# Windowed attention and a feed-forward layer on one core: batch 0 begun in groups of 256 tokens, two head pairs stacked on the partitions

## The chip, the cores and the metric

One core of a Trainium2 chip runs the whole program. Its engines work beside each other, each on its own instruction stream: PE (TensorE, matrix products and transposes), DVE (VectorE), ACT (ScalarE), POOL (GpSimd) and SP, which only issues transfers. ACT and POOL issue transfers as well. The metric is the device time of one execution in microseconds, as the median of several runs.

## The reference

There are 4 batches of 8 heads with 768 tokens and 64 numbers per head. A token sees itself and the 127 before it, and the first four tokens ("sinks"). The result goes through a layer of 512 to 2048, a squared relu, and back to 512.

```python
scores = scale * np.matmul(q, k.transpose(0, 1, 3, 2))
rel = pos[:, None] - pos[None, :]
keep = (pos[None, :] < 4) | ((rel >= 0) & (rel < 128))
scores = np.where(keep, scores, -1000000000.0)
a = np.exp(scores - np.max(scores, axis=-1, keepdims=True))
a = a / (np.sum(a, axis=-1, keepdims=True) + 1e-09)
x = np.matmul(a, v).transpose(0, 2, 1, 3).reshape(B * S, H * D)
out = np.maximum(x @ w_in, 0.0) ** 2 @ w_out
```

## The kernel before, in words

The kernel keeps both weight matrices in on-chip memory as bf16 and goes through the four batches one after the other. Within a batch the work is cut into groups of tokens (GROUPS, lines 323 to 325: batch 0 has one group of 512 and one of 256 tokens), and within those into stretches of 256 tokens (s = 0, 1, 2). Heads go in pairs (m = 0 to 3), so that two heads fill 128 partitions.

For batch 0 the start runs like this:

- **Loads.** load_qk (line 328) loads one head pair's k or q for 512 tokens as one transfer of 256 KB in fp32, four tokens (1 KB) to a partition row, all on SP's queue; eight such transfers load the first group. The second group comes with load_cast (line 355) on POOL's queue, which turns it into bf16 on the way. load_v (line 372) and load_w_in (line 299) are on POOL's queue too. Line 417 loads the sink values (vs_in), for batch 0 on ACT's queue.
- **Regroup** (line 471): a cast to bf16 on DVE, ACT or POOL (tile qs).
- **Transpose** (line 488, matmuls on line 500): PE transposes 128x128 blocks into PSUM (tile pt). **Unload** (line 515): DVE or ACT copies them to qkT, and puts the tokens back in their order.
- **Scores** (line 590): for s = 0 a bias product (line 600) puts the mask in ahead of the products on line 607; ACT takes the exponential (line 628); for later s the mask is put on by DVE or POOL (line 633).
- **Values** (line 656, matmuls on line 676), **norm** on DVE (line 687), and the **bridge** (line 718): PE transposes the result, and DVE or ACT copies it to xT (line 734).
- **Layer 1** (line 746, matmuls on line 757) and layer 2 follow.

PE also runs matmuls whose result nobody reads (warm, line 178, matmuls on line 182). The table DUMMIES (line 56) says how many stand ahead of which operation, by the operation's number.

Every piece of work is an operation of a Plan, numbered in the order in which the code makes it. The text ORDER (lines 21 to 55) lists these numbers in the order in which they are handed to the engines, each with a letter for its engine (p PE, d DVE, a ACT, g POOL; none means the first that is named) and, behind a plus, a choice of buffer. The engines run their instructions strictly in this order and wait on semaphores for each other. The framework counts transfers of SP and ACT on eight semaphores in turn; an issue waits until the last transfer on its semaphore has landed.

The constants are made by fill (line 220), fill_first and fill_second (lines 232 and 235) on DVE and by build_ident, build_triangles, build_bias and build_head_rows (lines 238 to 264) on POOL.

Of the kernel before, what the change touches and what calls it, by code (L numbers as in the profile page):

```python
# [21 lines left out]
0 7 8 9 1 5 10 11 2 12 13 3 14 15 55d 57+0 16 19 59a 20 17 56d 21 18 61d 63+0 22 58 62d 65a 60d 64 6 67a 83+1 79 66a  # L22
68d 69+1 85 70 71d 103+0 84+0 105 73g 74d 72d 23 75+1 86 76 77d 91+0 78a 24 87+1 93 25 89 88 92+0 80 26 114+1 90 94
95+0 4 96 117 97 106g 99+1 98 104+0 107 100d 101 118g 81+1 102d 113+0 108d 156 115 127 27 28 29 30 31 32 33 34 35 36
37 38 116d 82 109+0 111 39 40 41 119+1 121 157a 158a 110 112 120 122 162 123+1 125 163d 168 169d 126a 124a 171 172a
170a 159 160d 177 128 131 165 173d 161d 132d 178d 166d 164a 130a 129a 133a 144 146 136 138 174 145 137 289 290 148
134 175a 140 135 176a 147d 167d 139d 291 179d 292 293 141d 142 143 149g 42 43 44 45 46 150 151 47 48 49 50 51 52 53
54 365 366 367 368 208g 369 370 371 372 373 294 295 152 154 296 153d 155d 297d 298d 186 187d 180 181a 200+0 204+1
192+0 201 193 205 194a 206d 195a 189 207d 182d 203a 196+0 197 183 198a 190a 191a 188d 199d 202d 274 212+0+0 184d 209
278 279 215 213 237+0+0 210+1 211 238 240 185d 300 301 275 214 302 241d 276 277 303 280 281 282 304 219+0+0 283 222  # L30
220 306a 305 307 230+0+0 309a 233 231 308 311 223 216 221 310 239d 224+0 312 234g 232g 299 385 386 384 383 313 225
314 242+0 217+0 243 218 284 315 316 235+0 236 285 251+0 286a 287a 317d 252d 253d 244+0 246 226+1 228 247d 227d 245a
248+1 229a 399 322 249d 250d 402 400 323d 355 401 256+0+0 259 257 340 254+0 255 341a 258d 358 356 342a 396 260d 334
335a 374 375 376 377 378 379 380 381 395g 388 390 387 288 392 391 318 389 393 394 331 263+0+0 332a 261+1 264 266 319
262 267d 324d 406 333a 407 320a 337 409 265g 382 597 268+0 598 599 600 601 602 603 604 605 606 607 608 609 610 338a
321d 403 269 328 627d 410 270+0 272 404 408 329a 271a 273d 359 325 405 339a 336a 326a 346 347d 357 327a 415 418 419d
330d 352 411 353a 416 412 354d 447 448 343 344a 345a 349 422 423 425 417g 426g 611 451 452 397 363 449 453d 350d 398
450 351a 348a 454 455 457 466 456a 438 458 459 441 439 467 485 486 489 490 487 460 488 461 361 492 431 491a 432 434
615 413 616 622 620 619 493 462 494d 468 463 464a 414 465 621 617 618 420 440g 612 424g 427 496 433g 442g 428 498
421 470 471 443 435g 436 472a 504a 495 362 499 497 500 473 444 437 508 505 469 628 501 475d 474 477 647 429 625 445  # L40
430 446 650 502a 648 624 503 623 626 360 476 478 481 507 479 506 480 364 482 483d 523+0 525a 524 631 527 526 528 634
632 509+0 510 529 511d 512 530 531a 654 538 633 539 513 514 515 655 533 534 657 649g 656g 516 517a 638 613 614 535
635 536d 537 641 519 520 532a 636 658g 651g 521 639 569+0 570 637 571a 629 583+0 630 572 573 585a 640 522a 518a 574
584 587 575 576 586 555+1 642 589 577a 588 643 679 557a 540 556 590 559 591a 592a 578a 558 560 579 580 593 594 581
561 562 595 541+0 542 683 563a 564a 543d 545 544 680 546 565 547 566 548 684 686 644 567 685a 596a 549a 582a 681
550d 689 682 645 484 646 670 551 552 687 690 673 671 674g 553 688a 554a 663 691 694 666 664 665g 568d 698 692 693
699 659 652 702 703 705 667g 672g 695 696d 700 653 717 660 718 721 668 697 661 736a 704a 669 737 675 676 701 722 739
740 738 708 677 678 662 755+1 706 709 741+1 742 757a 719 720 756 743a 723a 707d 759 745 724 758 761 725 744 760 762
763a 764a 711 746 727 710 713 726a 765 766 747 712 769 714 771 767 728 730 715d 772 748 749a 729 815+0 816 817a 732
770 731 818 733 819 751 752 787+1 734a 735 716 801+0 802 803a 789a 753 820 804 768d 821 788 822 773+1 805 791 754a  # L50
823a 824a 775a 790 806 750d 792 829 807 774 793 776 825 808 794 826 809a 827 830 831 795a 796a 810a 777 779 811 778
812 797 798 833 780 834 836 813 799 828a 835a 781a 832 838d 839 783 784 782a 800a 814a 837 840 841 844 785 786d 842
848 849 852 853 855 843 845 846d 867 854a 850 851 858 857d 868 871 847 856 859 873a 861 862 860 863 864 869 872 865a
866 870 877 874 876a 875 878 880 881 886 879 882 883 885 884
# [59 lines left out]
def kernel(  # L114
# [112 lines left out]
    def fill_one(i):  # L227
        nc.vector.memset(kblk[i], 0.0)
        nc.vector.memset(vs_sb[i], 0.0)
        nc.vector.memset(v_sb[i][:, :, :, D:D + 1], 1.0)  # L230
# [4 lines left out]
    def fill_second(e):  # L235
        fill_one(1)

# [28 lines left out]
    bias_slot = Slot("sg", 4)  # L266
    c_const = op(-9, {"dve": 0.85}, fill, takes=[bias_slot])
    c_fill = op(-8.9, {"dve": 0.95}, fill_first, after=[c_const])
# [30 lines left out]
    def load_w_in(i, behind=None, yields=()):  # L299
        c = slice(512 * i, 512 * i + 512)  # L300
        w_in_op[i] = dma_op(
            "pool", ("w_in", i),
            lambda e: [nc.gpsimd.dma_start(out=w_in_sb[:, i],
                                           in_=moe_w_in[:, c].rearrange("(a p) f -> p a f", p=128))],
            2.6, behind, yields=yields)
        w_in_op[i].margin = 0.4 + 0.4 * i
# [17 lines left out]
    GROUPS[0] = [(0, 4), (512, 2)]  # L324
    GROUPS[1] = [(0, 4), (512, 2)]
    ROW = {512: 0.03, 1024: 0.052}

    def load_qk(b, m0, ti, g, pairs=2, behind=None, yields=()):


        t0, n = GROUPS[b][g]
        shares = 4 // pairs if n == 2 else 2 if pairs == 1 else 1
        half, share = m0 // pairs % shares, ("share", b, g, ti, m0 // (pairs * shares))
        if not half:
            qr_slot[share] = Slot("qr", 4 if n == 2 and pairs == 1 else 2)
        for m in range(m0, m0 + pairs):
            qr_slot[b, m, ti, g] = qr_slot[share]

        def run(e):
            if half == 0:  # L340
                qr_t[share] = bank(qr_slot[share], "qr", [128, shares * 2 * pairs, n * D], FP32)
            t = qr_t[share][:, 2 * pairs * half:2 * pairs * half + 2 * pairs, :]
            qr_t[b, "all", m0, ti, g] = t
            for m in range(m0, m0 + pairs):
                qr_t[b, m, ti, g] = t[:, 2 * (m - m0):2 * (m - m0) + 2, :]
# [6 lines left out]
        for m in range(m0, m0 + pairs):  # L352
            ops["qk", b, m, ti, g] = o
# [931 lines left out]
```

## Time and profile before

| | us |
|---|---|
| median of the runs | 213.04 |
| the runs | 213.04, 212.20, 213.47 |
| the profiled execution | 211.87 |
| its span, first to last instruction | 210.17 |
| mean granted clock of PE | 0.997 |

Line 2 of the next block is PE's busy share in 40 equal slices of the span, in tenths (9 is 90% or more); the others are DVE, ACT and POOL in the same way.

```
PE   3999999999999999999999999799999999999993
DVE  7487567366999964789997988999989978999863
ACT  2498287407744579898952268889870244896110
POOL 7999774898877941999369023700253000000000
```

A line of the chain of waits has the start, the length and what ran; a line of the timeline has the start, the length, the engine, the source line and the tiles, and in brackets the idle time before it and what ended it. A "q" behind an engine's name means that its sequencer issued a transfer.

### The profile page before, as it was taken

What the parts mean: (1) busy time and instruction counts of PE and PEld (TensorE: products, weight loads), DVE (VectorE), ACT (ScalarE), POOL (GpSimd) and SP (SyncE); (2) the same over time, 40 slices, a digit from 0 to 9 for tenths busy, and PEclk for the clock granted to TensorE, in tenths of its full rate; (3) what the DMA queues carried; (4) which work ended last, traced back from release to release, by engine and by line L of the source; (5) the groups of instructions that cost most, each with busy time, mean ns of one, the idle gap of its engine ahead of it and who ended that gap; (6) DMA issues with size and microseconds to landing.
All of it is one profiled execution on the core that took longest, in us unless ns stands there. A gap on an engine that the chain in (4) does not pass through costs nothing.

```text
span 210.2 us, 5719 instructions
## 1 busy us (share of the span) xinstructions
PE 201.4 (96%) x2383; PEld 169.4 (81%) x2383; DVE 170.8 (81%) x317; ACT 126.6 (60%) x162; POOL 101.8 (48%) x143
## 2 busy tenths in 40 slices
PE   3999999999999999999999999799999999999993
PEld 3859996689468845679789988699899999999892
DVE  7487567366999964789997988999989978999863
ACT  2498287407744579898952268889870244896110
POOL 7999774898877941999369023700253000000000
PEclk9999999999999999999999999999999999999998
DMA  5999999999999999999987639700512300400222
GB/s 171 278 188 206 171 201 214 161 155 205 153 112 157 104 150 252 138 124 144 149 102 151 103 77 179 50 3 0 150 62 69 75 5 38 166 0 0 103 100 100
DMA packets 93881, 26.09 MB, mean 124 GB/s; under 512 B 86816, under 2 KB 91552, under 8 KB 93856
## 3 DMA queue, kind: packets, MB, share of 16 engines
q0 software_dynamic: 69248, 12.59, 81.3%
q1 hardware_dynamic: 24424, 13.07, 27.9%
q8 instruction: 18, 0.29, 0.6%
q10 hardware_dynamic: 184, 0.07, 0.1%
q14 instruction: 7, 0.06, 0.1%
HBM read 27.30 MB, written 6.29 MB: 160 GB/s over the span
## 4 chain that ended last, share of the span: by engine, by line
PE 94%; DVE 2%; ACT 1%; POOL 1%; issue 1%; POOLq 0%; DVEq 0%
PE py L1086 29%; PE pm L757 20%; PE pm L887 17%; PE po L676 7%; PE py L976 7%; PE ps L607 6%; PE pt L500 3%; PE pt L182 2%; PE px L725 1%; ACT expm L628 1%; PE ya L1086 1%; PE ps L600 1%; PE pk L566 1%; DVE r L955 1%; DVE gT_sb L911 0%
## 5 line engine op out<-in xcount | busy, mean ns | idle before, releaser
L215 POOL TENSOR_SCALAR_AFFINE_SELECT expm<-expm 128x512 bf16<-128x512 bf16 x42 | 29.2, 724 | 49.5 <-ACT expm L628 24.5
L628 ACT ACTIVATE expm<-ps 128x1024 bf16<-128x1024 f32 (+1 forms) x48 | 43.8, 950 | 12.4 <-PE ps L607 11.3
L757 PE MATMUL pm<-xT,w_in_sb 128*128 128x256 bf16 (+1 forms) x320 | 44.7, 294 | 0.0
L757 PEld LDWEIGHTS <-w_in_sb 128*128 128x128 bf16 x320 | 34.2, 114 | 6.6 <-issue 0.9
L1086 PEld LDWEIGHTS <-gT_sb 128*128 128x128 bf16 x336 | 31.1, 98 | 4.2 <-issue 0.5
L1086 PEld LDWEIGHTS <-sg 128*128 128x128 bf16 x240 | 22.8, 98 | 3.3 <-issue 0.5
L768 ACT ACTIVATE r<-pm 128x1024 bf16<-128x1024 f32 x14 | 14.3, 1022 | 13.5 <-PE pm L757 13.4
L887 PEld LDWEIGHTS <-w_in_sb 128*128 128x128 bf16 x256 | 21.8, 114 | 0.5 <-issue 0.2
L887 PE MATMUL pm<-xs,wi 128*128 128x128 bf16 (+1 forms) x192 | 19.5, 246 | 1.5 <-DVE xs L845 0.9
L1086 PE MATMUL py<-wt,gT_sb 128*128 128x256 bf16 x160 | 20.8, 273 | 0.0
L1086 PE MATMUL py<-wt,sg 128*128 128x256 bf16 x160 | 20.6, 273 | 0.0
L909 ACT ACTIVATE gT_sb<-r 128x1024 bf16<-128x1024 bf16 x18 | 18.4, 1051 | 0.3
L1086 PE MATMUL py<-w_out_sb,gT_sb 128*128 128x256 bf16 x144 | 18.5, 273 | 0.0
L189 ACT ACTIVATE osb<-py 128x256 f32<-128x256 f32 (+1 forms) x15 | 6.2, 410 | 20.3 <-DMA out_dram<-osb 6.0
L770 DVE TENSOR_SCALAR r<-pm 128x1024 bf16<-128x1024 f32 x10 | 12.2, 1222 | 7.5 <-PE pm L757 4.3
L887 PEld LDWEIGHTS <-wi 128*128 128x128 bf16 x192 | 16.4, 113 | 2.2 <-issue 2.1
L693 DVE TENSOR_TENSOR xn_sb<-po,rc 128x512 bf16<-128x512 f32 (+1 forms) x28 | 17.2, 615 | 1.0
L676 PEld LDWEIGHTS <-expm 128*128 128x128 bf16 x352 | 16.3, 97 | 1.4 <-issue 0.5
L676 PE MATMUL po<-v,expm 128*128 128x65 bf16 x352 | 17.3, 193 | 0.1
L943 ACT ACTIVATE r<-pm 128x1024 bf16<-128x1024 f32 x12 | 12.1, 1021 | 8.1 <-PE pm L887 7.9
L928 DVE TENSOR_TENSOR t<-t,pm 128x512 f32<-128x512 f32 x24 | 15.9, 680 | 0.9 <-ACT t L189 0.4
L955 DVE CUSTOM_DVE_ANT_1 r<-pm,t 128x1024 bf16<-128x1024 f32 x12 | 14.5, 1220 | 1.6 <-PE pm L887 1.5
(97 smaller groups left out, 381.9 us busy)
## 6 DMA issues: line engine op xcount, KB each, us to landing
out_dram<-osb SPq DMA_DIRECT2D x11, 512.0 KB, 4.5
v<-in_v_dram POOLq DMA_DIRECT2D x24, 128.0 KB, 7.1
qn<-in_k_dram POOLq DMA_DIRECT2D x20, 128.0 KB, 7.1
qn<-in_q_dram POOLq DMA_DIRECT2D x20, 128.0 KB, 6.9
w_in_sb<-in_moe_w_in_dram POOLq DMA_DIRECT2D x4, 512.0 KB, 10.2
w_out_sb<-in_moe_w_out_dram POOLq DMA_DIRECT2D x4, 512.0 KB, 10.4
qr<-in_k_dram SPq DMA_DIRECT2D x4, 256.0 KB, 5.1
qr<-in_q_dram SPq DMA_DIRECT2D x4, 256.0 KB, 4.8
```

The costliest lines, as they stand in the source:

```text
L215: nc.gpsimd.affine_select(out=e_tile, in_=e_tile, compare_op=ALU.is_ge, fill=fill, base=i - 1, pattern=[[0, n], [1 if i else -1, 128]], ch ...
L628: nc.scalar.activation(out=x[:, :, o:512], in_=bank_t["s", b, s, m][:, :, o:512], func=AF.Exp, scale=scale)
L676: touch(("po", b, s, m0), e, nc.tensor.matmul(pv[:, i, h2, :], lhsT=lhsT, rhs=rhs, start=(n_ == 0), stop=(n_ == len(mms) - 1)), j)
L693: touch(("po", b, s, m0), e, nc.vector.tensor_tensor(out=xn_sb[:, 2 * s:2 * s + 2, 128 * (m0 + j0):128 * (m0 + j0 + nj)].rearrange("p i (j ...
L757: nc.tensor.matmul(pm[:, i, :], lhsT=w_in_sb[:, fb // 4, kb, fb % 4:512:4], rhs=xT[:, c0 // 256:(c0 + cw) // 256, kb, :], start=(kb == 0), ...
L768: nc.scalar.activation(out=o, in_=h, func=AF.Relu)
L887: touch(tag, e, nc.tensor.matmul(y[:, bk, i, :], lhsT=weights(name, f0 + i, a), rhs=rhs[:, a, :], start=fresh and i == 0 and a == 0, stop= ...
L909: nc.scalar.activation(out=d, in_=x, func=AF.Square)
L928: touch(tag, e, nc.vector.tensor_tensor(out=T["t"], in0=T["t"], in1=T["y"][:, bk], op=ALU.subtract), bk)
L955: touch(tag, e, nc.vector._custom_dve(TENSOR_ADD_SAT, out=r.rearrange("p b n c -> p b (n c)"), in0=T["y"].rearrange("p b n c -> p b (n c)" ...
L976: touch((b, u), e, nc.tensor.matmul(pm[:, i, :], lhsT=gT_sb[:, fb, 128 * t:128 * t + 128], rhs=w_out_sb[:, fb, :], start=(fb == 0), stop=( ...
L1086: ins = nc.tensor.matmul(y_, lhsT=x[:, i, :], rhs=r_, start=(first or tail and n == 2) and i == 0, stop=i == HB - 1, skip_group_check=not ...
```

## The change

- Batch 0 is cut in three groups of 256 tokens. The first two are loaded by a new load_qk: for two head pairs at a time, one pair goes to partitions 0 to 63 and the other to 64 to 127, as two transfers of 128 KB in 1 KB rows. For the first group one of the two is on SP's queue and the other on ACT's; for the second group both are on SP's.
- A regroup, a transpose and an unload now handle two head pairs of 256 tokens, where they handled one pair of 512. Their number for the first 512 tokens stays as it was.
- The second group of 256 tokens has its sink scores of its own; the first has none.
- The memset of the ones in v_sb[0] stands ahead of all other constants, and the loads of the values wait for it alone. They are the first thing that POOL issues.
- The values of s = 0 no longer wait for the sink values. vs_in of batch 0 is loaded on SP's queue.
- ORDER is new throughout. DUMMIES stays as it is, while the numbers of the operations change.

```diff
+    def fill_ones(e):
+        nc.vector.memset(v_sb[0][:, :, :, D:D + 1], 1.0)
...
+    c_ones = op(-9.1, {"dve": 0.2}, fill_ones)
     c_const = op(-9, {"dve": 0.85}, fill, takes=[bias_slot])
...
-    GROUPS[0] = [(0, 4), (512, 2)]
+    GROUPS[0] = [(0, 2), (256, 2), (512, 2)]
...
+    def load_qk(m0, ti, g):
+        t0 = GROUPS[0][g][0]
+        if not m0:
+            qr_slot[ti, g] = Slot("qr", 2)
+        for half in range(2):
+            def run(e, half=half):
+                if not m0 and not half:
+                    qr_t[ti, g] = bank(qr_slot[ti, g], "qr", [128, 2, 2, 4 * D], FP32)
+                h0 = 2 * (m0 + half)
+                return [(nc.scalar if half and not g else nc.sync).dma_start(
+                    out=qr_t[ti, g][64 * half:64 * half + 64, m0 // 2],
+                    in_=(q, k)[ti][0, h0:h0 + 2, t0:t0 + 256, :].rearrange("h (p t) d -> p h (t d)", t=4))]
...
-            o.after.append(c_rest if b else c_fill)
+            o.after.append(c_rest if b else c_ones)
...
                     def regroup(e, m=m, ti=ti):
+                        t = qs_t[b, m, ti, g] = bank(qs_slot[b, m, ti, g], "qs", [128, 4, 2, D], BF16)
+                        copy(e, t, qr_t[ti, g][:, m // 2].rearrange("p h (t d) -> p t h d", d=D))
...
                             ins = copy(e,
+                                       qkT_sb[:, m:m + 2, j, t0 // 128:last // 128, :].rearrange(
+                                           "c i a b -> c i (a b)").rearrange("c i (p t) -> c i p t", t=4),
+                                       bank_t[b, m, g][:, j, 0:512].rearrange("c (t i p) -> c i p t", t=4, i=2))
...
-                                + [A["sink_values"]] + prev_bridge)
+                                + ([A["sink_values"]] if s else []) + prev_bridge)
...
-    load_sinks("act", 0)
-    for m in range(NP):
-        for ti in (1, 0):
-            load_qk(0, m, ti, 0, 1)
-    for b in range(1, B):
+    for g in range(2):
+        for m0 in (0, 2):
+            for ti in (1, 0):
+                load_qk(m0, ti, g)
+    for b in range(B):
         load_sinks("sp", b)
-    load_v(0, 0, None, [("qk", 0, 3, 0, 0)])
+    load_v(0, 0)
...
             at(0, 0.0, 1.0, ("den", "att"))
...
-            at(1, 0.2, 0.725, "att")
+            at(1, 0.0, 1.0, ("den", "att"))
+            at(2, 0.2, 0.725, "att")
```

More of the change, by code (lines that the diff above doesn't have):

```diff
@@ L323 @@
     GROUPS = {b: [(0, 6)] for b in range(B)}
-    GROUPS[0] = [(0, 4), (512, 2)]
+    GROUPS[0] = [(0, 2), (256, 2), (512, 2)]
     GROUPS[1] = [(0, 4), (512, 2)]
[L326 to L345, printed above, removed]
-            return [nc.sync.dma_start(
-                out=t,
-                in_=(q, k)[ti][b, 2 * m0:2 * m0 + 2 * pairs, t0:t0 + 128 * n, :].rearrange(
-                    "h (p t) d -> p h (t d)", t=n))]
-        o = dma_op("sp", ("qk", b, m0, ti, g), run, 16 * pairs * ROW[256 * n] + (0.7 if (b, m0, ti, g) == (0, 0, 0, 0) else 0.0), behind,
-                   () if half else [qr_slot[share]], yields)
-        for m in range(m0, m0 + pairs):
-            ops["qk", b, m, ti, g] = o
@@ L495, in transpose @@
                             for ti in part:
[L496 removed]
+                                for t in range(nt):
                                     o = 128 * n * ti if w == 2 else 0
```

119 lines of the change are left out of this document (53 added, 66 removed).

## The prediction, made before the changed kernel ran

> **What bounds the kernel now.** I read the page first, for the share of each engine, then the busy time by stretch, then the chain of waits, and last the timeline of the first 17 us.
>
> ```profile
> span 210.2 us, 5719 instructions
> PE 201.4 (96%) x2383; PEld 169.4 (81%) x2383; DVE 170.8 (81%) x317; ACT 126.6 (60%) x162; POOL 101.8 (48%) x143
> ...
> 0.00:16.83 16.83, 13.13 (x178) 10.17 (x179) 11.55 (x33) 9.82 (x14) 14.63 (x30) 1.00 1.24 212
> 16.83:130.00 113.17, 113.17 (x1341) 89.45 (x1341) 89.88 (x165) 71.62 (x91) 75.84 (x99) 1.00 1.69 155
> 130.00:135.00 5.00, 3.46 (x57) 2.91 (x54) 4.82 (x6) 4.39 (x6) 5.00 (x8) 1.00 0.95 78
> 135.00:206.70 71.70, 71.67 (x816) 66.85 (x812) 64.50 (x114) 40.46 (x53) 6.28 (x9) 1.00 0.18 56
> 206.70:210.20 3.50, 0.00 (x0) 0.00 (x0) 0.01 (x1) 0.28 (x1) 0.00 (x0) 0.83 0.45 150
> ```
>
> In the rows by stretch the columns are the stretch, its length, and busy us of PE, PE's weight loads, DVE, ACT and POOL. PE never rests from 16.83 to 130 and from 135 to 206.7. Its idle time is 3.5 us ahead of its first instruction, 1.54 us between 130 and 135, and the 3.5 us of the last stores. So a change of the start is worth what it moves the moment from which PE never rests, which is the first product of layer 1 (16.83), if the same work is done by then.
>
> ```profile
> 3.53 2.95 PE pt L182 x26
> 6.48 0.43 PE pt L500 x4
> 6.91 1.40 PE pt L182 x18
> 8.30 0.45 PE pt L500 x8
> ...
> 16.83 1.91 PE pm L757 x16
> ```
>
> These are lines of the chain of waits (start, us, what). The first 26 matmuls are the dummies of line 182: 2.95/26 = 113 ns each. The eight transposes at 8.30 take 56 ns each. The 18 dummies between take 78 ns on average, so the granted clock doubled among them: about n x 107 + (18 - n) x 56 = 1400 gives n = 8, which is 7.7 us, 4.1 us after PE began. PE started early on work that nobody needs and had its full clock when the real transposes came in numbers.
>
> ```profile
> 0.82 0.46 SPq L346 DMA_DIRECT2D qr<-in_k_dram  x1
> ...
> 2.13 1.28 ACT L189 ACT_TABLE_LOAD   x1 [2.13 <-issue]
> ...
> 5.65 0.43 DVE L191 CAST qs<-qr 128x512 bf16<-128x512 f32 x1 [0.60 <-DMA qr<-in_k_dram]
> ...
> 7.06 0.45 DVE L191 CAST qs<-qr 128x512 bf16<-128x512 f32 x1 [0.99 <-DMA qr<-in_q_dram]
> ...
> 10.06 2.50 ACT L628 ACTIVATE expm<-ps 128x768 bf16<-128x768 f32 x3
> ```
>
> In the timeline the casts show when loads of 256 KB land: the first four start at 3.60, 4.63, 5.65 and 7.06. ACT's table is loaded by 3.41, in the shade of the loads, and the first exponential starts at 10.06.
>
> **The change, part by part.** *Same work ahead of layer 1.* The listing of the built program puts 32 transposes, 8 bias products, 40 score products, 24 value products, 8 bridge transposes and 4 sink products ahead of the first layer 1 product in both kernels. So the work behind it (186 us of PE plus 1.54 and 3.5) is the same, and the sum is: time after = time before + (new start of layer 1 - 16.83) + change in later stalls.
>
> *Dummies.* DUMMIES still names the old operations. In the new numbering 57, 63, 64, 83, 91 and 97 are loads, a regroup, norms and a copy, which call no warm; only 101 (3) and 119 (2) do. 58 of 63 dummies go. Their time itself (about 4.5 us at 107 and 56 ns) lay ahead of real work and costs nothing, but PE now begins with the first real transposes, at about 5.7. With the 4.1 us that the trace shows from first matmul to full clock, the full clock comes at 9.8, and until then a transpose takes 107 and not 56 ns.
>
> The Trainium skill (TensorE: Matmul & The Clock Gate, Part 1) has a free-running window of about 3.4 us that must be busy, which by 5.7 would put the full clock between about 9.1 and 12.5, an estimate. The trace's 4.1 us fits it.
>
> *Loads.* The same 256 KB steps in 1 KB rows now hold two head pairs of 256 tokens. One queue already moved 290 GB/s from 4 to 6 us and 353 from 6 to 7 with the 16 DMA engines at a busy share of 1.01 and 1.03, so the second queue gives no rate. Values first: in the record of DMA packets the pool queue's first packet came 1.6 us after the issues at 67.4, 84.5 and 130.8, and 3.9 us after the very first at 3.43. From the new issue at 1.07 that is 2.7 to 5.0, in the midst of the q and k loads. I take the early end with a third of the bandwidth: first landings 3.65 (k), 5.0 (q), 6.3 (k), 7.5 (q), against 3.60, 4.63, 5.65, 7.06 without. The second group (9.0, 10.6, 12.0, 13.4) then shares with w_in block 0. Values land by about 8.2, not 12, and nobody asks for them before 13.6.
>
> The Trainium skill (DMA: Bandwidth & Descriptors, Rules for kernel authors) says of halves on two queues that they share the same engines; if the queues added up instead, the first pair would land some 0.5 us sooner, and so would the sum.
>
> *ACT, which now ends last.* It issues four loads (SP's rows: 0.46 to 0.56 each, so until 2.9; had the first cost the 1.28 of ACT's one issue before, 3.7). In the listing the table load now waits for the first ACT load: 3.7 to 4.98, 1.57 later than before. Behind it stands everything: two casts (0.62 each, second ready 6.22); wait for PE's transposes of q (4 x 107 ns and 0.2 to drain) to 6.96; unload 0.60 to 7.56; wait for four score products at half clock to 8.35; exponential 0.82; unload to 9.77; wait for the next scores to 10.62 (their transposes wait for q at 7.5 and DVE's 0.79 of fills and 0.43 of cast, then bias and scores 1.2 at half clock); then without a pause exponential, exponential, unload, exponential (to 13.68), two exponentials of 1.03, two unloads of 0.60: 16.94. In sum 4.98 + 9.58 of work (2 x 0.62, 5 x 0.60, 4 x 0.82, 2 x 1.03) + 2.38 of waits (0.74, 0.79, 0.85). PE's sink products (0.22) and last 12 scores (0.66) stand between this and layer 1: **17.87, or 1.04 late**. ACT's copy of xT (to 17.5) and w_in 0 lie in that shade. Had the clock been full from the first, the same chain gives 17.2; with it at 9, 17.3; at 11, 18.0; at 12, 18.4; at 13, 19.2.
>
> *Other moves.* POOL: both value issues (2.1 us) go ahead of the identity (3.47 to 4.0, wanted at 5.7) and the bias (3.23 to 6.6, wanted at 6.7: cover of 0.1, each us beyond it counts whole). Its cast for the second group waits for its load (9.0), and behind it stand two values (to 11.6), w_in 1 (12.4, was 12.0), casts, w_in 2 and 3 (15.7, was 13.5). Block 1 is asked for at 21; from 12.4 and the 8.2 to 12.0 us that such loads took to land it comes at 20 to 24: nothing, up to 3. Sink values move from 9.6 to 18.4, wanted at 19.6. vs_in on SP, behind 12 loads, lands ahead of that. Of DVE's six casts three go to ACT (one more) and POOL (two more); its first memset (0.10) has 2 us of slack behind it.
>
> *Later.* The order is new throughout, the products are the same. The one stall of PE (1.54 us at 130 to 135, PE behind DVE's xs, line 845) may go; DVE is busy 64.5 of 71.7 us beyond it, so new ones can come. Bounds -1.5 to +3; I take 0.
>
> **Sum.** 211.87 (the profiled execution, 1.67 around its span) + 1.04 = 212.9; the median of the runs stands 1.17 above that execution, so **214.1**.
>
> **Rivals.** *The gate opens late.* PE begins with gaps, and a gap in a window may cost the next whole wait. With full clock at 13 layer 1 starts at 19.2: 215.4. Against: on half clock the chain keeps PE busy some 90% from 5.7 to 11. The same would come of a gate that transposes don't open, but the first 7.7 us of the trace hold nothing else, and it opened.
> The Trainium skill (same page, Part 4) says that transposes don't count as busy; here the clock was granted at 7.7 us after transposes alone.
>
> *The stall at 130 goes.* In the new listing DVE's two xs sums over xT stand ahead of a mask and two subtractions, earlier than before, and PE's wait of 0.86 on them would go, and with it the 0.68 behind ACT: 214.1 - 1.5 = 212.6, not slower; with a clock at 9, 212.0. For it: the place is plain in the listing. Against: DVE has as much to do there.
>
> *A new stall of DVE or of w_in* in the replanned order, 1 to 3 us: 215 to 217. For it: PE has no slack anywhere, and ACT ends the first batch's exponentials at 20.0, not 17.85.
>
> *It does what it says:* the first exponential comes at 8.35, 1.7 sooner than 10.06, and layer 1 with it at 15.1: 211.3. Against: ACT's 9.58 of work from 4.98 on, with even half of the waits, is 15.8, and 0.9 of PE follows: 16.7 at best.
>
> **How the numbers follow.** Forecast 0.38, with its own range 213.3 to 214.9 (clock at 9 to 12); late gate 0.16; new stall 0.20; stall gone 0.20; as named 0.06. A change of 0.5% (1.07 us) is about what a measurement of this kernel, whose three runs spread over 1.27, can tell from none. Faster than 211.97: all of the last and half of the stall gone: 0.16. Slower than 214.11: half of the forecast, the late gate and nearly all of the new stall: 0.53. Within: 0.31. Range: 212.0 to 216.5.
>
> **What would show it.** Right: the table load at 3.6 to 3.8; transposes 107 ns apart until 9 to 12; the first exponential at 8 to 8.7 and the last of the first eight after 17; layer 1 at 17.3 to 18.4 with PE busy on from there. Wrong: the table load ahead of any landing; full clock before 8; layer 1 before 16.8; or PE idle in a place after 20 that outweighs the start.

## The result, and the profile after

| | before | after |
|---|---|---|
| median of the runs, us | 212.98 | 219.87 |
| the runs | 213.04, 212.20, 213.47, 212.92 | 220.90, 220.16, 219.57, 219.58 |
| the profiled execution | 211.87 | 220.90 |
| its span | 210.17 | 219.20 |

The ratio is 1.034, with a 95% interval of 1.029 to 1.038: slower, and 5.8 us above the forecast of 214.1. The two profiled executions differ by 9.0 us and the medians by 6.9: before's, 211.87, lies below all its other times, and after's, 220.90, is the longest of its four. Where a place is read from these two traces, some 2 us of the difference are of that kind. One trace below, of before in halves, is of an execution in a slower state (225.63 us at a granted clock of 0.93, where the others took 220.95 to 221.28), and only its issues and packets are read.

The head of the page of after and its busy time by stretch (columns as before: stretch, length, PE, PE's weight loads, DVE, ACT, POOL; then PE's clock, the DMA engines' busy share, GB/s):

```profile
span 219.2 us, 5600 instructions
PE 202.0 (92%) x2325; PEld 166.8 (76%) x2325; DVE 172.8 (79%) x321; ACT 123.0 (56%) x158; POOL 97.6 (45%) x137
...
0.00:22.97 22.97, 12.77 (x119) 7.51 (x120) 9.73 (x29) 11.05 (x16) 14.78 (x31) 1.00 1.07 173
22.97:134.70 111.73, 111.73 (x1313) 87.82 (x1310) 89.94 (x168) 68.06 (x87) 70.88 (x91) 1.00 1.55 144
134.70:142.00 7.30, 5.75 (x89) 5.07 (x87) 7.06 (x9) 5.66 (x7) 6.34 (x8) 1.00 0.85 55
142.00:215.70 73.70, 71.75 (x812) 66.37 (x811) 66.03 (x117) 38.03 (x50) 5.65 (x9) 1.00 0.26 69
215.70:219.20 3.50, 0.00 (x0) 0.00 (x0) 0.00 (x0) 0.21 (x1) 0.00 (x0) 1.00 0.47 156
```

Layer 1 starts at 22.97 instead of 16.71 (its first weights; the products follow at 23.04 and 16.83). That is 6.3 of the 9.0 us. Behind it the stall in the middle kept its size (7.30 - 5.75 = 1.55, before 1.54), and the last stretch has 1.95 us of idle PE where before had 0.03. PE's 2,214 matmuls behind the start are busy 0.9 us longer than the same number before; no run tells why.

The chain of waits ahead of layer 1:

```profile
1.64 6.14 DMA qr<-in_q_dram
...
7.80 7.45 DMA qr<-in_q_dram
...
15.37 0.87 DVE qs L191
...
16.29 0.61 PE pt L487 x4
16.90 0.64 PE ps L582 x2
17.54 1.28 PE ps L589 x10
...
21.65 0.62 PE px L707 x8
...
22.49 0.55 PE ps L589 x12
```

and three lines of before's, which from 3.53 on was PE but for two exponentials on ACT:

```profile
12.56 0.27 PE ps L607 x4
...
13.94 0.82 ACT expm L628
...
15.75 1.03 ACT expm L628
```

Two transfers of q make up 13.6 of the first 15.3 us: SP's half of the first q load of the first group (issued 1.64), and the second half of the first q load of the second group, whose issue on SP waited for the semaphore of that transfer. Ten score products take 1.28 us at 17.54, 128 ns each, where products of the same size in before take 0.27 us for four, 68 ns each: PE had full clock only from 21.25 on, by the clock record of the trace (before: 7.6). The clock column of the stretches says 1.00 from the start, because it takes the time ahead of that record's first entry as full. (The twelve products at 22.49 are half as wide.)

The timeline of ACT and DVE in the first 12 us:

```profile
0.81 0.72 ACTq L340 DMA_DIRECT2D qr<-in_k_dram  x1
...
4.22 1.28 ACT L189 ACT_TABLE_LOAD   x1 [4.22 <-DMA qr<-in_k_dram]
...
7.87 0.63 ACT L189 ACTIVATE qs<-qr 128x512 bf16<-128x512 f32 x1 [1.73 <-DMA qr<-in_q_dram]
...
10.39 0.81 ACT L610 ACTIVATE expm<-ps 128x768 bf16<-128x768 f32 x1 [0.59 <-PE ps L589]
```

and of DVE alone:

```profile
8.82 0.43 DVE L191 CAST qs<-qr 128x512 bf16<-128x512 f32 x1 [1.29 <-DMA qr<-in_k_dram]
...
11.44 0.43 DVE L191 CAST qs<-qr 128x512 bf16<-128x512 f32 x1 [1.35 <-DMA qr<-in_q_dram]
```

The table load and each of these casts start when a load has landed. The first k pair is there at 4.2, q at 7.8, k at 8.7 and q at 11.3; before, four loads of the same size were there at 3.60, 4.63, 5.65 and 7.06.

The DMA engines show what became of the loads. Busy time by stretch (the last two columns are the share of the 16 DMA engines' time that packets took, where packets of several queues overlap above 1, and GB/s), first before:

```profile
2.00:4.00 2.00, 0.47 (x5) 0.47 (x6) 1.75 (x6) 1.28 (x1) 1.88 (x5) 1.00 0.92 281
4.00:8.00 4.00, 4.00 (x44) 4.00 (x42) 1.92 (x4) 0.60 (x1) 3.85 (x7) 1.00 1.05 306
```

then after:

```profile
2.00:4.00 2.00, 0.00 (x0) 0.00 (x0) 0.75 (x3) 0.00 (x0) 1.84 (x5) 1.00 0.72 178
4.00:8.00 4.00, 0.61 (x4) 0.34 (x4) 0.69 (x1) 2.04 (x3) 3.08 (x8) 1.00 1.43 199
8.00:12.00 4.00, 2.37 (x15) 1.21 (x16) 1.63 (x4) 2.39 (x4) 0.00 (x0) 1.00 1.26 226
```

From 2 to 4 us the engines are not even full (0.72). From 4 to 8 they are taken more than before (1.43 against 1.05) and move less (199 against 306 GB/s). By the record of DMA packets 1,769 packets of these four us are the values', of 128 bytes and 32 ns each, beside 555 packets of q and k of 1 KB, most of 46 to 59 ns; in before 112 and 1,180 started. PE, with nothing to do, is busy 0.61 us of these four, where before it was busy all the time.

### The profile page after: what moved, and what is told of

It reads as the page before. It is cut to its first block, busy times and chain, and to the rows that moved or that the text cites. A ratio compares the mean times of both kernels' runs of the same rounds, so it can differ in the third digit from the quotient of the medians.

```text
span 219.2 us, 5600 instructions
## 1 busy us (share of the span) xinstructions
PE 202.0 (92%) x2325; PEld 166.8 (76%) x2325; DVE 172.8 (79%) x321; ACT 123.0 (56%) x158; POOL 97.6 (45%) x137
## 4 chain that ended last, share of the span: by engine, by line
PE 83%; DMA 9%; DVE 5%; issue 1%; SPq 0%; ACT 0%; DVEq 0%
PE py L1068 25%; PE pm L739 20%; PE pm L869 15%; PE py L958 7%; PE po L658 6%; DMA qr<-in_q_dram 6%; PE ps L589 5%; DMA out_dram<-osb 2%; PE pt L487 2%; PE px L707 1%; DVE r L937 1%; DVE xn_sb L675 1%; PE pk L548 1%; DVE t L910 1%; DVE gT_sb L893 0%
## 5 line engine op out<-in xcount | busy, mean ns | idle before, releaser
L610 ACT ACTIVATE expm<-ps 128x1024 bf16<-128x1024 f32 (+1 forms) x48 | 43.7, 953 | 19.2 <-PE ps L589 19.2
L215 POOL TENSOR_SCALAR_AFFINE_SELECT expm<-expm 128x512 bf16<-128x512 bf16 x30 | 21.3, 735 | 55.6 <-ACT expm L610 48.2
L750 ACT ACTIVATE r<-pm 128x1024 bf16<-128x1024 f32 x18 | 18.4, 1024 | 10.6 <-PE pm L739 9.4
L869 PE MATMUL pm<-xs,wi 128*128 128x128 bf16 (+1 forms) x192 | 20.0, 246 | 1.3 <-DVE r L937 1.2
L1068 PE MATMUL py<-w_out_sb,gT_sb 128*128 128x256 bf16 x144 | 18.7, 273 | 0.0
L658 PEld LDWEIGHTS <-expm 128*128 128x128 bf16 x352 | 16.9, 100 | 1.4 <-issue 0.5
L658 PE MATMUL po<-v,expm 128*128 128x65 bf16 x352 | 17.8, 197 | 0.0
L891 ACT ACTIVATE gT_sb<-r 128x1024 bf16<-128x1024 bf16 x17 | 17.5, 1053 | 0.3 <-DVE r L937 0.2
L622 DVE TENSOR_TENSOR expm<-expm,tri 128x1024 bf16<-128x1024 bf16 x17 | 13.8, 820 | 3.7 <-ACT expm L610 3.7
L925 ACT ACTIVATE r<-pm 128x1024 bf16<-128x1024 f32 x11 | 11.1, 1023 | 8.7 <-PE pm L869 7.9
L761 DVE TENSOR_TENSOR gT_sb<-r 128x1024 bf16<-128x1024 bf16 x18 | 12.7, 716 | 3.7 <-ACT r L750 3.5
L958 PE MATMUL py<-w_out_sb,gT_sb 128*128 128x512 bf16 x64 | 15.5, 380 | 0.0
## 6 DMA issues: line engine op xcount, KB each, us to landing
w_out_sb<-in_moe_w_out_dram POOLq DMA_DIRECT2D x4, 512.0 KB, 10.6
```

Of the source, the lines that this page charges most:

```text
L215: nc.gpsimd.affine_select(out=e_tile, in_=e_tile, compare_op=ALU.is_ge, fill=fill, base=i - 1, pattern=[[0, n], [1 if i else -1, 128]], ch ...
L610: nc.scalar.activation(out=x[:, :, o:512], in_=bank_t["s", b, s, m][:, :, o:512], func=AF.Exp, scale=scale)
L622: nc.vector.tensor_mul(y, y, tri.rearrange("p (o a) c -> p o (a c)", o=1).to_broadcast([128, 4, 256]))
L658: touch(("po", b, s, m0), e, nc.tensor.matmul(pv[:, i, h2, :], lhsT=lhsT, rhs=rhs, start=(n_ == 0), stop=(n_ == len(mms) - 1)), j)
L750: nc.scalar.activation(out=o, in_=h, func=AF.Relu)
L869: touch(tag, e, nc.tensor.matmul(y[:, bk, i, :], lhsT=weights(name, f0 + i, a), rhs=rhs[:, a, :], start=fresh and i == 0 and a == 0, stop= ...
```

## The experiments

Theory A: the values' transfers, issued first, take the engines' time ahead of q and k. Theory B: loads of 128 KB in halves on 64 partitions are slow of themselves. Theory C: the late clock costs by itself. The ratios are to runs of the kernel before on the same chip (212.6 to 212.9).

**Values later** (218.71; ratio 1.029, 1.026 to 1.031). In ORDER the two value loads (28, 29) and block 0 of w_in (23) move behind the bias and the identity:

```diff
-... 15 0 28 29 1 16 17 18 19 20 21 22 3 7 4 23 24 25 26 30 6 5 99g
+... 15 0 1 16 17 18 19 20 21 22 3 6 4 28 29 23 24 25 26 30 7 5 99g
```

> After, with the two value loads and block 0 of w_in issued behind the bias and the identity on POOL's queue (from about 3.4 us, as in before), and nothing else moved. Theory A (small packets of the values' loads, in flight from 3.5 us on, slow the q and k loads): the last q of the first group lands at 8 to 9 us instead of 11.3, the second group's q by 12.5 instead of 15.25, layer 1 starts at 19 to 21 instead of 22.97, time 216.5 to 218. Theory B (the halves on two queues, not the values, slow the loads): layer 1 at 22.5 to 23.5, time 219.4 to 220.4. Theory C (the granted clock alone): landings may be earlier, but full clock still comes near 21 us and layer 1 not before 21.5, time 218.5 to 219.5.

Here the values' first packet came at 6.40. The first group was there by 8.2, but the second group's last packet still came at 15.60, since the values' and w_in's packets met it instead. Layer 1 came at 20.79.

**One queue** (220.11; 1.036, 1.033 to 1.038).

```diff
-                return [(nc.scalar if half and not g else nc.sync).dma_start(
+                return [nc.sync.dma_start(
```

> After, with both halves of every load on SP's queue, none on ACT's. Theory A (the values slow the loads): landings within 0.7 us of those of after, layer 1 at 22.3 to 23.6, time 219.2 to 220.5; ACT's table load comes first thing, before any landing. Theory B (two queues of halves disturb each other): the 16 engines end one transfer within 0.8 us of each other instead of up to 2.4, the first group's last q lands by 9, layer 1 at 20 to 21, time 217 to 218.

Layer 1 at 23.48. It is not the second queue that disturbs.

**Warm** (218.50; 1.028, 1.025 to 1.031).

```diff
-    57: 26, 63: 18, 64: 3, 83: 3, 91: 3, 97: 5, 101: 3, 119: 2,
+    66: 18, 67: 18, 72: 8, 73: 24, 101: 22, 102: 30, 119: 2,
```

> After, with 63 dummy products put back where PE waits for the first group's loads (ahead of the transposes and scores of its four head pairs) so that PE is busy from the first load on; loads as in after. If the late full clock (21.25 us in after) costs of itself: full clock at 9 to 13, layer 1 at 20.5 to 21.7, time 217.4 to 218.6. If the loads alone set the start (the second group's q lands at 15.25 and about 6.3 us of work follow, little of it on PE): full clock early, but layer 1 at 22.4 to 23.2, time 219.2 to 220.2.

Full clock at 8.5, and layer 1 at 22.75 all the same. The 1.4 us came from behind layer 1 (194.2 us to the end instead of 196.2): PE's wait for an output store near the end was gone. (The table calls 122 products, not 63; see below.)

**Before, values first** (215.09; 1.011, 1.008 to 1.014).

```diff
-0 7 8 9 1 5 10 11 2 12 13 3 14 15 55d 57+0 16 19 59a 20 17 56d
+0 7 8 9 10 11 12 13 14 15 19 20 1 5 2 3 55d 57+0 16 59a 17 56d
...
+        nc.vector.memset(v_sb[0][:, :, :, D:D + 1], 1.0)
```

(the new line in fill; the loads then wait for fill alone)

> Before, with the ones of the first value tile written first and the two value loads issued first on POOL's queue (about 1.5 us instead of 3.4), everything else of before kept: loads of 512 tokens, one queue. Theory A (early values slow the q and k loads): q and k of the first group land 1 to 2.5 us later than the 3.60 to 7.06 of before, layer 1 at 18 to 19 instead of 16.83, time 214 to 215.5. Theory B (only the halves on two queues do): layer 1 within 0.4 us of 16.83, time 212.5 to 213.5.

Layer 1 at 20.14, later than the 18 to 19 that was expected, and 2.5 us on the median: theory A holds in the kernel before, with nothing else of the change in it. (The identity was built later too, at 5.69 instead of 3.19, but the chain of waits is q's last load until 14.07.)

**Before without the warm-up** (212.94; 1.001, 0.998 to 1.004).

```diff
-    57: 26, 63: 18, 64: 3, 83: 3, 91: 3, 97: 5, 101: 3, 119: 2,
+    101: 3, 119: 2,
```

> Before, with 58 of its 63 dummy products left out (those that ran from 3.5 to 9 us while the loads were under way), nothing else changed; it prices the warm-up alone. If the warm-up is worth what the prediction reckoned (the clock some 4 us later): full clock at 9 to 12 instead of 7.6, layer 1 at 17.5 to 19 instead of 16.83, time 213.2 to 215. If it is worth nothing because the loads set the pace: layer 1 within 0.4 us of 16.83, time 212.2 to 213.

In the profiled executions the full clock came at 13.15 instead of 7.6 and layer 1 at 18.15 instead of 16.71; the medians don't differ beyond the interval (-0.4 to 0.9 us). So the 58 lost dummies alone cost nothing that the medians show as long as the loads come in time, though the full clock came 8.4 us after PE's first transposes (4.76), not 4.1.

**Before in halves** (221.25; 1.040, 1.036 to 1.044) and **before split by heads** (219.07; 1.029, 1.026 to 1.032).

```diff
-            return [nc.sync.dma_start(
-                out=t,
...
+            return [nc.sync.dma_start(out=t[64 * x:64 * x + 64], in_=src[64 * x:64 * x + 64])
+                    for x in range(2)]
```

and for the second

```diff
+            return [nc.sync.dma_start(out=t[:, pairs * x:pairs * x + pairs], in_=src[:, pairs * x:pairs * x + pairs])
+                    for x in range(2)]
```

> Before, with each of its eight q and k loads of 256 KB split into two of 128 KB (64 partitions each), all on SP's queue; nothing else changed. If small loads cost rate by themselves (16 issues of 0.6 us, 128 KB each): the last q of the first group lands at 8 to 9.5 instead of 7.06, the last load at 12 to 13 instead of 10.8, layer 1 at 17.8 to 19, time 213.8 to 215.5. If the engine time of the packets alone counts: landings within 0.6 us of before, layer 1 at 16.6 to 17.4, time 212.3 to 213.3.

> Before, with each of its eight q and k loads split into two of 128 KB by heads (all 128 partitions, 128 rows of 1 KB each), on SP's queue. If the number of issues costs (16 of 0.6 us each): landings as in the run of before with halves (first group's last q near 10.8, last load near 18), time 219 to 221. If it is the form of 64 partitions and two heads: an issue takes under 0.45 us, landings within 1 us of before, layer 1 at 16.8 to 17.8, time 212.5 to 213.7.

The same bytes in 16 loads instead of 8 cost the kernel before 8.5 us (64 partitions), more than the whole change, or 6.4 us (128 partitions, one head each). The timeline of SP in halves,

```profile
0.81 1.44 SPq L348 DMA_DIRECT2D qr<-in_k_dram  x2
2.29 1.25 SPq L348 DMA_DIRECT2D qr<-in_q_dram  x2
```

and by heads:

```profile
2.86 0.91 SPq L348 DMA_DIRECT2D qr<-in_k_dram  x2
```

An issue of 128 KB on 64 partitions takes mostly 0.61 us, one on 128 partitions 0.43, hardly less than the 0.45 to 0.47 of 256 KB before. So a queue offers at most 128/0.65 = 197 KB per us in halves and 128/0.48 = 267 by heads, with the gaps between issues. Both runs have the last load at 16 to 18 us, since POOL's packets now came in among them from 5.5 on (before: 7.33, from the same issues at 3.4). The price of an issue is not the whole of it: the form by heads has cheap issues and still lost 6.4 us. Part of both losses is the clock: in the run by heads it was full from 7.62, at half from 14.45 to 21.28, and full again, and layer 1 came at 23.97.

**Before in halves, values behind the loads** (222.85; 1.049, 1.045 to 1.053): as in halves, and

```diff
-    load_v(0, 0, None, [("qk", 0, 3, 0, 0)])
+    load_v(0, 0, ("qk", 0, 3, 0, 0))
```

> Before with halves of 64 partitions, and POOL's first value load, with block 0 of w_in and all later loads behind it, issued only once the first group's last q load has landed. It parts the 8.5 us of the run of before with halves into the issues alone and the collision with the values. If the issues alone count (16 of 0.65 us): first group landed by 7.5, second group by 12.5 to 13, layer 1 at 18 to 19.5, time 214 to 215.8. If the values' packets in the same engines make up nothing of it: second group at 16 to 18 again, time 219 to 221.

In this kernel that load is the last of all eight, not of a first group, so POOL stood still until 13.99 and its cast behind it made PE wait 7.7 us. Its time says nothing. Its loads do: alone on the engines they ran at 193 KB per us, the pace of the issues, and ended at 13.0 instead of 17.8.

**Late and warm** (218.58; 1.029, 1.025 to 1.034) and **values behind the first group, warm** (217.75; 1.025, 1.021 to 1.029). The first joins the edits of values later and of warm; in the second the first value load, and all of POOL's loads behind it, wait for the first group's last q (and stand behind the bias and the other constants in ORDER):

```diff
-    load_v(0, 0)
+    load_v(0, 0, ("qk", 0, 3, 0, 0))
```

> After, with the values and block 0 of w_in issued at 3.4 us as in the run of values later, and the 63 dummy products put back as in the warm run. If the two costs add: layer 1 at 18.8 to 20.0 instead of 20.8 (values later alone) and 22.8 (warm alone), full clock from 9 on without the half-clock stretch of 16 to 19.6, time 215.2 to 216.8. If the loads of the second group alone set layer 1: 20.4 to 21, time 217 to 218.

> As the run before it, but POOL issues the first two value loads, and block 0 of w_in behind them, only once the first group's last q load has landed (7 to 8 us). Theory A (the values' 4.1 us and block 0's 3.1 us of all 16 DMA engines stand ahead of the q and k loads, and order alone decides): first group landed by 7.5, the second group by 11 to 12 instead of 16, layer 1 at 17.3 to 18.5, time 213.2 to 214.8. Theory B (sixteen loads of 128 KB, their issues and their waits for a free semaphore hold the second group): the second group still lands after 13, layer 1 at 19.3 or later, time 215.5 or more.

Layer 1 at 22.38 and at 21.73, though in the second the last packet of q and k came at 12.35. Its chain of waits shows what I had built in:

```profile
10.02 1.34 PE pt L182 x24
...
12.88 1.33 PE pt L182 x22
14.22 0.22 PE pt L487 x4
14.44 1.68 PE pt L182 x30
```

Dummies (line 182) between transposes whose data had long landed. So these two runs, and warm, tell nothing of the price of the clock, and I took most dummies out.

**Values behind, no dummies** (217.32; 1.020, 1.014 to 1.025) and **with 26 of them** (215.84; 1.014, 1.012 to 1.017).

```diff
-    57: 26, 63: 18, 64: 3, 83: 3, 91: 3, 97: 5, 101: 3, 119: 2,
+    66: 18, 67: 8, 101: 3, 119: 2,
```

(the second; the first keeps the table of after)

> As the run of the values behind the first group, without the 122 dummy products of the warm-up (which in that run ran at full clock from 6.7 to 16 us between transposes whose data had landed, 6.3 us of PE's time): after, with only the issues of the values and of block 0 of w_in moved. Theory A (order of the transfers decides): landings as there (first group 7.5, second group 11.8), layer 1 at 17.5 to 19.5, block 0 of w_in landing at 17.1 being the floor, time 214.5 to 216.5. If something else than the dummies held that run at 21.8: layer 1 at 21 or later, time 217.5 to 218.5.

> The same with 26 dummy products ahead of the first two pairs' transposes, where PE only waits. If the late full clock still costs with the loads out of the way: full clock at 7 to 8.5, layer 1 0.7 to 2 us earlier than in the run without dummies, at 17.2 to 18.2, time 213.8 to 215. If the clock costs nothing: layer 1 within 0.4 us of the run without.

Layer 1 at 19.10 and 18.58: theory A holds. (The last q and k came later than the 11.8 that the expectation took over: their last packets at 14.14 and 12.71, since the values still met the last of them.) At layer 1 the early clock (full at 7.84 against 13.45) is worth at most 0.5 us here, since the last packets came sooner too; the other 1 us of the medians is of the size of the wait for the store at the end (1.6 us in the first's trace), which the second does not have. What still makes the second's PE wait are the late values and w_in (us in all, times, longest):

```profile
PE po L658 <- DMA v<-in_v_dram: 1.2, 2, 0.8
PE pm L739 <- DMA w_in_sb<-in_moe_w_in_dram: 0.5, 2, 0.3
```

**26 dummies alone** (217.85; 1.024, 1.019 to 1.029) and **with the values at 3.4 us** (216.39; 1.017, 1.013 to 1.021): the table above in after, and in values later.

> After with 26 dummy products ahead of the transposes of the first two pairs, where PE only waits for loads; issues and loads as in after. It prices the late clock alone, without the 122 products that stood in the way in the warm run, and it shifts the program by as many instructions as the run of 26 dummies with the values behind, where PE's wait for the output store at the end was gone. If the clock costs: full clock at 8 to 12 instead of 21.25, layer 1 at 20.5 to 22. If the loads alone set the start: layer 1 at 22.4 to 23.2. If the wait at the end hangs on where the instructions lie: no wait for osb over 0.5 us, and layer 1 to the end in 194.2 to 195.3 instead of 196.2. Time 216.8 to 218.9.

> After with the values and block 0 of w_in issued at 3.4 to 6.3 us (as in the run of values later) and the 26 dummy products. Beside the run with the values behind the first group (215.84), only the issue of the values differs. If the order of transfers decides: the second group lands at 14.5 to 16 against 12.6 there, layer 1 at 19.3 to 20.5 against 18.58, time 216.5 to 217.8. If landings of the second group don't matter once the clock is early: 215.5 to 216.3.

Layer 1 at 21.86 and 20.59. With the loads of after the early clock is worth 1.1 us at layer 1, though it fell back to half from 11.9 to 18.7, after PE had waited 1.5 us for the cast of a load ahead of 11.24. Behind layer 1 the trace of 26 dummies alone is 2.0 us shorter than after's (194.2 against 196.2), of which the store's wait is 1.83; by the medians the two kernels differ by 2.0 in all.

**Block 0 of w_in behind the last q** (221.00; 1.038, 1.034 to 1.042), **the same without the values**, and **eight issues on each queue** (222.62; 1.046, 1.041 to 1.050).

```diff
-    load_w_in(0)
+    load_w_in(0, ("qk", 0, 3, 0, 1))
```

for the second also

```diff
+                if b == 0 and t < 2:
+                    return []
```

and for the third

```diff
-                return [(nc.scalar if half and not g else nc.sync).dma_start(
+                return [(nc.scalar if half else nc.sync).dma_start(
```

(In ORDER block 0 also stands behind the other constants in the first two. The second fills the values' places with ones, so it leaves the attention of batch 0's first 256 tokens out.)

> After, with the values first as it has them, and block 0 of w_in issued only once the last q load has landed. It parts the two kinds of software transfers. If the values' packets cost the most: the first group as late as in after (last q 11.3), the last load at 13.5 to 14.5 instead of 16.4, block 0 landing at 18 to 20, layer 1 at 20.5 to 22. If block 0 costs the most: the last load at 12 to 13, layer 1 at 19.5 to 20.5. If neither: the last load at 16 again, layer 1 at 23 or later.

> As the run with block 0 of w_in behind the last q load, and the first two value tiles are not loaded at all (their part of v is written with ones on DVE, so the attention of batch 0's first 256 tokens is left out of the result). The q and k loads then have the 16 DMA engines to themselves. If the values' packets cost their engine time (64 packets of 32 ns on each engine for each tile, 4.1 us): the last load at 10 to 11 instead of 14.28, the first group's last q by 7.7 instead of 10.58. If the issues and the waits for a free semaphore cost of themselves: the last load at 12.5 to 13.5. Layer 1 at 17.5 to 19, held by block 0, which lands 5 us behind the last q load; time 214.5 to 216.5.

> After, with the second halves of the second group's loads on ACT's queue too (eight issues on each queue instead of 12 and 4). If SP's issues of 0.6 us for 128 KB, and the waits for a free semaphore among them, are what lets the values' packets in: the last load at 13 to 14.5 instead of 16.4, while ACT's table load begins at 6.2 to 7.5 instead of 4.2, and the first exponential 1 to 2 us later than 10.39; layer 1 at 21 to 23. If only the values' place in the order counts: the last load at 16 to 16.8, layer 1 at 23 to 25, time 219.5 to 222.

The first moved the last packet of q and k from 16.01 to 13.74, the second to 11.09. The second has only two times, 217.91 and 224.31. In the third the loads came no sooner (15.41), and ACT, whose issues waited for semaphores, began late:

```profile
10.36 1.28 ACT L189 ACT_TABLE_LOAD   x1 [10.36 <-DMA qr<-in_k_dram]
```

The transfers in one table, from the record of DMA packets (us; KB of q and k, of 2,048, still to come when the first packet of POOL's queue moved):

| kernel | POOL's first packet | still to come | last packet of q, k | layer 1 |
|---|---|---|---|---|
| before | 7.33 | 481 | 10.35 | 16.71 |
| before, values first | 4.22 | 1,492 | 13.64 | 20.14 |
| before, by heads | 5.60 | 1,286 | 16.29 | 23.97 |
| after | 3.47 | 1,773 | 16.01 | 22.97 |
| values later, 26 dummies | 6.67 | 1,005 | 15.94 | 20.59 |
| values behind, 26 dummies | 9.58 | 308 | 12.71 | 18.58 |
| w_in 0 behind | 3.47 | 1,766 | 13.74 | 23.17 |
| the same, no values | 13.46 | 0 | 11.09 | 19.44 |

Once POOL's packets flow, q and k get 98 to 172 KB per us in the runs of this table (77 to 194 over all), whatever the form and the number of queues. Before them they get 290 in the kernel before, 206 to 250 in halves on two queues, 160 to 193 in halves on one. (In the last two rows POOL stands still until it may issue w_in 0, at 14.56 and 11.81, and its cast behind that issue makes PE wait, 1.58 and 1.07 us; w_in 0 itself landed at 19.97 and 17.38, ahead of layer 1. So their layer 1 and times carry that wait, and only their loads are used.)

**Before with fewer dummies** (212.32; 0.998, 0.996 to 1.000), as a version that might beat both:

```diff
-    57: 26, 63: 18, 64: 3, 83: 3, 91: 3, 97: 5, 101: 3, 119: 2,
+    57: 26, 63: 8, 101: 3, 119: 2,
```

> Before, with 29 fewer of its 63 dummy products: the 10 last of the 18 ahead of the second pair's transposes (they run at 6.9 to 8.3 us, after the data have landed) and 19 of the single ones that follow; the first 26, which run while PE only waits, stay. If they stand in the way: layer 1 0.3 to 1 us earlier than 16.83, time 211.7 to 212.4, faster than both kernels. If PE had nothing else to do, or the clock comes later for it: 212.4 to 213.

It does, by 0.2%, less than a difference that is worth the name here. Layer 1 did not come earlier in the profiled execution (16.89 against 16.71). The best version with groups of 256 tokens stayed 3.2 us behind the kernel before.

## Why the prediction was wrong

**The step that failed is Loads.** It took the pace of the new loads from rows of other loads: "One queue already moved 290 GB/s", and the values' packets at "a third of the bandwidth". The first packet of the values did come at 3.47, within the 2.7 to 5.0 that it gave. But q and k then got 141 KB per us, half of the 290 instead of two thirds. The landings, forecast and measured, and those of the run without values, where none of POOL's packets moved before 13.46:

| | k | q | k | q | k | q | k | q |
|---|---|---|---|---|---|---|---|---|
| forecast | 3.65 | 5.0 | 6.3 | 7.5 | 9.0 | 10.6 | 12.0 | 13.4 |
| measured | 4.15 | 7.79 | 8.72 | 11.32 | 13.50 | 15.25 | 15.73 | 16.43 |
| without values | 4.16 | 5.74 | 6.71 | 7.63 | 8.57 | 9.53 | 10.48 | 11.52 |

So for the first four loads the forecast was 0.1 to 0.7 us ahead even of loads that had no packets of POOL's beside them: it had given the halves and the values together no price there.

By the runs, the last packet's 5.66 us over the kernel before (16.01 - 10.35) are 2.27 for w_in 0 (16.01 - 13.74), 2.65 for the values (13.74 - 11.09), and 0.74 for the halves, without POOL's packets, over before, which had POOL's packets beside its last quarter. At the 290 KB per us that before had until then, its last packet would have come at 9.0 without them (an estimate), so the halves' own price is nearer to 2.1. They also leave the door open: before had issued all its loads by 4.95 us and had a quarter left when POOL's packets began; after had issued six of twelve on SP by 5.3, and its seventh waited until 6.61 for one of the eight semaphores. Before in halves shows the same without the values being first (8.5 us). Why POOL's packets began at 5.5 and not 7.33 there, from the same issues, is not settled; that a deep queue of issued loads holds them back was only argued, and POOL's time from first issue to first packet goes from 2.4 to 3.0 us even among the three runs with the values at that time and the same issues (values later, late and warm, 26 dummies with it).

The Trainium skill (DMA: Bandwidth & Descriptors, Rules for kernel authors) advises against two transfers to disjoint partition halves, because both share the same engines, and for one transfer over 128 partitions. The runs agree, and cost it at far more than the prediction made of it; two loads over all 128 partitions instead of one cost 6.4 us as well, so the halves are not the only point. The same page (Issuing engines are not separate DMA queues) holds the time to initiate a transfer to be usually small beside the transfer; here it is 0.62 us for 128 KB, which at before's 290 KB per us move in 0.44.

**ACT, which now ends last.** The landings were its input, and so it failed with them: the table load began at 4.22 (forecast 3.6 to 3.8; an ACT issue took 0.62 to 0.72, not 0.46 to 0.56), the second cast at 7.87 instead of about 5.6, the first exponential at 10.39 (8 to 8.7), layer 1 at 22.97 (17.3 to 18.4). ACT did not end last: the chain is two q loads, then PE and DVE.

**Dummies.** The full clock, forecast at 9.8, came at 21.25. The 4.1 us from first matmul to full clock supposed that PE stays busy once begun; it was busy 0.61 us of the four from 4 to 8 us and 2.37 of the next four. The late loads are only part of that: with the first q and k in time the full clock still came at 12.6 to 13.5 without the dummies (no values, before without the warm-up, values behind). So this step failed of itself, and the rival of a late gate, priced for 13, was the better account: its sum gives layer 1 at 19.2, and the run of the values behind without dummies had 13.45 and 19.10, though its last load was later (14.75) than the sum supposes. The late clock's price at layer 1 is 1.1 us with the loads of after (the run of 26 dummies) and at most 0.5 with the values behind. That the dummies' own time costs nothing was right by the medians (before without the warm-up: 212.94). (By "same page" that rival means the page of the Trainium skill that the prediction cites under Dummies, not the one on DMA.)

**Other moves.** The bias' thin cover of 0.1 us never mattered, since q was later still. **Same work** held in number (2,214 matmuls behind the start in both traces); the 186 us that it gives for them are 188.3 by its own rows, and the chain of ACT with PE's two terms behind it adds up to 17.82, not 17.87, which moves the sum by 0.05. **Later** was taken as 0; the stall in the middle stayed as it was (1.55 against 1.54), and a new stall came, though not of DVE or w_in as in the rival: 1.83 us of PE ahead of 211.92, behind an output store.

**In sum**, by layer 1 from after to before: 22.97, 21.86 with 26 dummies, 20.59 with the values at before's time, 18.58 with the values behind the first group, 16.71. By medians 219.87, 217.85, 216.39, 215.84, 212.98; the first step holds the store's wait too. The last step, 2.9 us by the medians and 1.9 at layer 1, was not parted by a run: in the traces w_in 0 lands at 17.25, the table load comes 2.1 us later than before (4.21 against 2.13), and values and w_in make PE wait behind the start.

## What to carry to other kernels

Price a reshaped load by its own issue and packet size, not by the bytes of the old one: count the issues, what one takes on its queue, and how many may be in flight, and ask how much of the urgent data is already issued when the next queue's packets come. A transfer that nobody waits for yet is not free if it is put first: its packets take time of the same 16 engines, 32 ns for each of the values' 128-byte packets, and here 2.65 us of the last landing. A filler that hides a wait is only a filler while its data are missing; put back in the wrong place it becomes the chain itself.

## What the runs showed of the hardware

- **A late store beside a block of instructions.** In after, the store of 512 KB issued at 206.16 landed 5.17 us later, and PE waited for its buffer. The chain of waits:

```profile
206.16 5.17 DMA out_dram<-osb
...
211.92 2.78 PE py L1068 x24
```

and the DMA view from 206 to 212 us (40 slices; the second line in GB/s), with the queue of instructions below:

```profile
DMA  0000004998979995000001001000000000000000
GB/s 0 0 0 0 0 0 191 410 410 355 382 328 382 382 410 137 0 0 0 0 0 27 0 0 27 0 27 27 27 27 27 27 0 0 0 0 0 0 0 0
...
q8 instruction: 1, 0.02, 1.0%
```

The store is all but done at 208.4; one packet of 16 KB on the queue of instructions is under way from 208.30 to 209.24, and the last packets of the store trickle one by one until 210.9 (the single 27s). A wait of 1.0 to 1.8 us is in all seven kernels of this grouping in which such a block comes while the store is under way (after, values later, one queue, values behind without dummies, w_in behind, without values, eight issues each), and in none of the six with 26 or more dummies, where it comes before the store's packets or up to 0.5 us behind the last of them. That the block holds up the one DMA engine on which the trickling packets wait is argued from this: the record does not name the engines, and with one queue and with eight issues each the block begins 0.3 us after all but two of the store's packets.

- **The issue of a load depends on its form**: mostly 0.45 to 0.47 us for 256 KB on 128 partitions in two rows each, 0.43 for 128 KB on 128 partitions in one row, 0.60 to 0.65 for 128 KB on 64 partitions in two rows, on SP and ACT alike (a queue's first ones took 0.72 to 0.81).
- **The clock falls back** after a start that went well: with 26 dummies it was full from 8.5, at half from 11.9 to 18.7, and full again; ahead of 11.24 PE had waited 1.53 us for the cast of a load that came late.
